# Mamba-2 scan and Hardswish layer: the order of the first loads and of the work up to the feed-forward

## The chip, the cores and the metric

The kernel runs on one core of a Trainium2 chip. The metric is the device time of one execution in microseconds; before the change the median of three runs is 336.48 us (336.34 to 337.1). A profile comes from one further execution, taken by the hardware profiler. Its engines are PE (TensorE; PEld is its weight load), DVE (VectorE), ACT (ScalarE), POOL (GpSimd) and SP (SyncE, which here only issues DMAs). ACT issues DMAs too.

## The reference

Batch 4, 8 heads, sequence 768, head width 32, state width 16, chunks of 32 in the reference. Within a chunk, with `cum` the running sum of log a:

```python
L = np.exp(cum[:, :, :, None] - cum[:, :, None, :]) * causal
y_intra = np.einsum('bhij,bhjd->bhid', np.einsum('bhin,bhjn->bhij', Cc, Bc) * L, xc)
y_inter = np.einsum('bhin,bhnd->bhid', Cc, state) * np.exp(cum)[:, :, :, None]
y[:, :, sl] = y_intra + y_inter
state = decay_full[:, :, None, None] * state + np.sum(Bx, axis=2)
```

The result, as 3072 tokens of 256, goes through a feed-forward layer with 2048 inner columns:

```python
h = x @ w_in
g = h * np.clip(h + 3.0, 0.0, 6.0) / 6.0
return (g @ w_out).astype(np.float32)
```

x, a, B and C are float32; the two weight matrices are float64.

## The kernel before

**Stages.** The sequence is cut into six chunks of 128 positions (`NC = 6`), each for all 4 batches at once, so that a chunk is 512 tokens. Chunk c is scanned (decays, scores, `mix`), and its 512 tokens go through the feed-forward as stage k = c, while the next chunk's scan is woven in. The order of every engine's instructions is written out by hand (`tc.manual_schedule()`): each engine runs its own in the order of the source, and waits where a result is missing. Semaphores are placed by the framework; eight are used for DMAs in turn, so that a ninth DMA waits for the first to land.

**The weights.** `w_in` and `w_out` arrive as float64 bits in eight parts of 1 MB (`load_w`, L144; parts 0 to 3 are `w_in`, 4 to 7 `w_out`), in three buffers `raw`. `decode(i)` (from L190) turns a part into float32: ACT copies the top 16 bits into `ws` (L202), DVE builds the significand in `wm` (L207, L211), masks exponent into `we` and sign into `ws` (L221, L223), ACT maps the exponent in two steps (L227, L230), DVE joins (L234) and multiplies into `w_in` or `w_out` (L244). `decode` is a generator; `weights(i, n)` runs n further pieces of it.

**The head, for chunk 0.** a is loaded first (L83). ACT issues the first weights and B, loads its function table (L150), and then copies and exponentiates; SP issues C in eight loads (`pairs_first`, L103), x (L121), and the second weights. DVE clips a (L284), ACT takes Ln (L286), DVE scans (L289) and splits the sum into three bfloat16 rows in `split` (L296 to L300, `in_three`). PE lays masks in PSUM (L370, L378), and adds differences of sums: `diff_less` (L383) and `diff_pick`, either with sixteen narrow products a batch (L399) or with two wide ones against `spread`, which DVE makes (L279, L391). ACT exponentiates to `L` (L407). C is transposed by DVE (L507) and masked by head (L517), B by PE (L464) with ACT's copy (L473). `scores` (L572) forms C B, `into_state` (L590) B x, `multiply` (L606, L616, L621) copies the state's halves (`adds`, `mid`) and multiplies `L` by the scores, `mix` (L667, L545) gives y, and `keep` (L683) copies it to `yT`. 30 one-column products (L365) and two `busy` products (L535) on PE have no use for the result.

**The first feed-forward stage.** `mlp_in(0, f)` (L693) for f = 0 to 15 multiplies `yT` by 128 columns of `w_in` in two products of 512 columns; the last 18 of the 32 are halved. The four banks f0 to f3 take turns, so that f waits for DVE to be done with f - 4. ACT makes the ramp (L796) and DVE the product `gT` (L801). Parts 2 to 5 are decoded in between: part i is needed from f = 4 i on while i < 4. `first_out` (L814) follows.

Of the kernel before, what the change touches and what calls it, by code (L numbers as in the profile page):

```python
# [21 lines left out]
def kernel(  # L22
# [65 lines left out]
    def load_bc(c):  # L88
# [41 lines left out]
    def load_w(i, queue=nc.sync):  # L130
# [58 lines left out]

    def decode(i):  # L190
# [10 lines left out]
        for sl in (slice(0, n),) if i != 1 else (slice(0, n // 2), slice(n // 2, n)):  # L201
            nc.scalar.copy(out=s[:, sl], in_=top[:, sl])  # L202
            if i == 1 and sl.start == 0:
                yield
# [20 lines left out]
        next(parts_m, None)  # L225
# [5 lines left out]
        if i and i + NRAW < 2 * NP:  # L231
# [23 lines left out]
    spread = [pre[:, 11 + c].bitcast(BF16).rearrange("k (h i) -> k h i", h=NH) for c in range(2)]  # L255
    of_batch = const.tile([P, NB], BF16, name="of_batch")
    of_head = const.tile([P, NH], BF16, name="of_head")
# [4 lines left out]
    def row_signs():  # L262
        with nc.allow_low_precision("zeros and ones"):
# [3 lines left out]
            nc.vector.tensor_reduce(  # L267
                out=of_batch, in_=pick.rearrange("k (b h) -> k b h", b=NB), axis=AX.X, op=ALU.add)
            nc.vector.tensor_reduce(
                out=of_head, in_=pick.rearrange("k (b h) -> k h b", b=NB), axis=AX.X, op=ALU.add)  # L270
# [5 lines left out]

    def spread_rows(c):

        nc.vector.tensor_tensor(  # L279
            out=spread[c], in0=split[:, c].unsqueeze(1).to_broadcast([P, NH, P]),  # L280
            in1=of_head.unsqueeze(2).to_broadcast([P, NH, P]), op=ALU.mult)
# [1105 lines left out]
```

## Time and profile before

| | |
|---|---|
| runs: median (lowest to highest) | 336.48 us (336.34 to 337.1) |
| the profiled execution: its time, its span | 337.3 us, 335.6 us |
| PE, PEld busy | 327.6 us (98%), 272.8 us (81%) |
| DVE, ACT, POOL busy | 264.2 us (79%), 208.2 us (62%), 130.3 us (39%) |
| first L693 product | 21.73 us |
| first L814 product | 49.39 us |
| DVE, ACT busy from 21.73 to 42.30 us | 18.95 us, 18.27 us of 20.57 |
| granted TensorE clock | 1.00 |

The span runs from the first to the last instruction; the device time has 1.7 us more around it. The profile has these views: a page with busy time by engine, slices, DMA queues and the costliest groups; the chain of work that ended last, followed back from the end; waits by engine and line; a timeline, in which neighbours of one kind are merged; and tables by stage with busy time and DMA share. L numbers are lines of the kernel before. A duration of a matmul includes its drain, so that neighbours overlap: the start of the next tells the pace.

### The profile page before, as it was taken

Reading aid. Unit: us, or ns where it says so; the run is one execution under the profiler, and the core shown is the slowest. Engines: PE = TensorE matmul, PEld = TensorE weight load, DVE = VectorE, ACT = ScalarE, POOL = GpSimd, SP = SyncE. Lnnn points to the kernel's source line nnn. Section 1 sums busy time; section 2 is a strip of 40 time slices with the busy share of each in tenths; the row PEclk is TensorE's granted clock in tenths of the full one; section 3 lists DMA queues with packets and bytes.
Section 4 is the critical chain, followed back from the end, with each engine's and each line's share of the span. In section 5 each row is a group of like instructions: output and inputs, shape, how many; then the busy total and the mean of one; then the engine's idle time right before and its main releaser. Section 6 shows DMA issues by size and latency. Waiting matters only on the chain.

```text
span 335.6 us, 8329 instructions
## 1 busy us (share of the span) xinstructions
PE 327.6 (98%) x3361; PEld 272.8 (81%) x3361; DVE 264.2 (79%) x418; ACT 208.2 (62%) x448; POOL 130.3 (39%) x125
## 2 busy tenths in 40 slices
PE   7989999999999999999999999999999999999995
PEld 5554888888888888887888888888888888899995
DVE  6879999879599639869949558938678958599973
ACT  4778887657987570677662577643487221677661
POOL 2200000280743896089973078771058740000000
PEclk9999999999999999999999999999999999999999
DMA  8979960684930214239107258100151001210001
GB/s 174 158 275 212 215 237 9 154 107 126 197 37 4 60 48 109 41 51 96 42 2 163 35 76 77 33 4 11 28 75 14 2 4 17 29 20 0 2 0 63
DMA packets 90181, 25.22 MB, mean 75 GB/s; under 512 B 82784, under 2 KB 86528, under 8 KB 89632
## 3 DMA queue, kind: packets, MB, share of 16 engines
q1 hardware_dynamic: 85760, 23.39, 36.9%
q10 hardware_dynamic: 4384, 1.31, 1.8%
q8 instruction: 26, 0.43, 0.5%
q14 instruction: 11, 0.09, 0.1%
HBM read 21.33 MB, written 3.29 MB: 73 GB/s over the span
## 4 chain that ended last, share of the span: by engine, by line
PE 90%; DVE 4%; DMA 3%; issue 1%; SPq 1%; ACT 1%; DVEq 0%
PE h L757 31%; PE wc L1005 8%; PE wb L1005 8%; PE o L814 8%; PE h L693 8%; PE wa L1005 7%; PE o_end L969 6%; PE wb L1013 3%; PE y L667 3%; PE y L545 2%; DVE q_part L897 2%; DMA raw<-in_moe_w_in_dram 2%; PE cb L572 2%; DVE gT L801 1%; DMA pairs<-in_C_dram 1%
## 5 line engine op out<-in xcount | busy, mean ns | idle before, releaser
L801 DVE SCALAR_TENSOR_TENSOR gT<-gT,h 128x512 f32<-128x512 f32 x96 | 64.7, 683 | 22.0 <-ACT gT L796 20.7
L796 ACT ACTIVATE gT<-h,half 128x512 f32<-128x512 f32 x96 | 65.5, 684 | 24.3 <-PE h L757 21.1
L777 ACT ACTIVATE h<-h 128x512 f32<-128x512 f32 x66 | 38.3, 585 | 37.0 <-PE h L757 36.7
L757 PE MATMUL h<-y_hi,w_part 128*128 128x512 f32 x160 | 50.9, 403 | 0.0
L757 PE MATMUL h<-y_less,w_part 128*128 128x512 f32 x160 | 50.1, 399 | 0.0
L757 PE MATMUL h<-y_lo,w_part 128*128 128x512 f32 x160 | 49.5, 395 | 0.0
L860 POOL TENSOR_TENSOR s<-gT 128x512 f32<-128x512 f32 x16 | 25.3, 1582 | 51.5 <-DVE gT L801 51.5
L757 PEld LDWEIGHTS h<-y_lo,w_part 128*128 128x128 f32 x160 | 30.0, 188 | 6.9
L757 PEld LDWEIGHTS h<-y_hi,w_part 128*128 128x128 f32 x160 | 30.1, 188 | 6.7
L757 PEld LDWEIGHTS h<-y_less,w_part 128*128 128x128 f32 x160 | 29.1, 188 | 6.2 <-DVE h L774 0.3
L427 ACT ACTIVATE L<-L,cum_n 128x64 f32<-128x64 f32 x128 | 31.7, 337 | 1.8 <-POOL L L162 1.8
L814 PE MATMUL o<-w_out,gT 128*128 128x256 f32 x128 | 28.8, 381 | 0.0
L693 PE MATMUL h<-yT,w_in 128*128 128x256 f32 (+1 forms) x100 | 27.8, 440 | 0.0
L814 PEld LDWEIGHTS o<-w_out,gT 128*128 128x128 f32 x128 | 24.1, 190 | 3.4
L693 PEld LDWEIGHTS h<-yT,w_in 128*128 128x128 f32 x100 | 18.9, 190 | 8.6 <-issue 5.7
L860 POOL TENSOR_TENSOR gT<-gT 128x512 f32<-128x512 f32 x16 | 23.9, 1500 | 0.7
L897 DVE TENSOR_TENSOR q_part<-gT,q_part 128x256 fp32r<-128x256 f32 x24 | 21.5, 923 | 0.1
L969 PE MATMUL o_end<-v_pair,g_pair 128*128 128x256 f32 x120 | 21.1, 281 | 0.0
L346 POOL TENSOR_SCALAR cum_n<-cum_t 128x128 f32<-128x128 f32 x1 | 0.5, 534 | 51.9 <-DVE cum_t L344 51.9
L162 POOL TENSOR_SCALAR_AFFINE_SELECT L<-L 64x1024 f32<-64x1024 f32 (+1 forms) x16 | 19.2, 1210 | 3.5 <-DMA L<-cum_d 3.1
L860 POOL TENSOR_TENSOR s<-s,gT 128x512 f32<-128x512 f32 x16 | 20.6, 1292 | 0.0
L438 POOL TENSOR_TENSOR bs<-B,L 128x128 f32<-128x128 f32 x24 | 12.1, 528 | 21.7 <-ACT L L427 14.2
(163 smaller groups left out, 636.2 us busy)
## 6 DMA issues: line engine op xcount, KB each, us to landing
raw<-in_moe_w_out_dram SPq DMA_DIRECT2D x4, 1024.0 KB
L<-cum_d SPq DMA_DIRECT2D x8, 512.0 KB
xt<-in_x_dram SPq DMA_DIRECT2D x6, 512.0 KB
raw<-in_moe_w_in_dram SPq DMA_DIRECT2D x3, 1024.0 KB
out_dram<-back SPq DMA_DIRECT2D x128, 16.0 KB
pairs<-in_C_dram SPq DMA_DIRECT2D x40, 32.0 KB
B<-in_B_dram SPq DMA_DIRECT2D x5, 256.0 KB
eto<-cum_e SPq DMA_DIRECT2D x20, 64.0 KB
```

Source lines behind the costliest of these rows:

```text
L162: nc.gpsimd.affine_select(out=t[rows], in_=t[rows], pattern=pattern, compare_op=ALU.is_ge, fill=-1e5, base=base, channel_multiplier=-1)
L427: nc.scalar.activation(Ls[c][:, b, h], Ls[c][:, b, h], AF.Exp, bias=cum_n[:, c, g:g + 1])
L693: nc.tensor.matmul(out=h[:, t:t + n], lhsT=w_in[f // FP][:, j, f % FP * P:(f % FP + 1) * P], rhs=yTs[k][:, j].rearrange("p b i -> p (b i)" ...
L757: nc.tensor.matmul(out=hs_[k, f], lhsT=w[j][:, f % FP * P:(f % FP + 1) * P], rhs=y[:, j], start=(start and j == 0), stop=True, skip_group_ ...
L777: nc.scalar.activation(h, h, AF.Copy, scale=1.0 / EPS + 1.0)
L796: nc.scalar.activation(gTs[k][:, f], h, AF.Relu, bias=half, scale=1.0 / 6.0)
L801: nc.vector.scalar_tensor_tensor(out=g, in0=g, scalar=1.0, in1=h, op0=ALU.min, op1=ALU.mult)
L814: nc.tensor.matmul(out=o[:, b % 2], lhsT=gTs[0][:, f, b * P:(b + 1) * P], rhs=w_out[:, f], start=(f == 0 and b % 2 == 0), stop=True, skip_ ...
L860: nc.gpsimd.tensor_tensor(out=o, in0=p_, in1=q_, op=op)
L897: nc.vector.tensor_tensor(out=l[:, j], in0=g[:, j], in1=h[:, j].bitcast(FP32), op=ALU.subtract)
L969: nc.tensor.matmul(out=ends_["cross" if n == 2 else "squares"][b], lhsT=g_parts[t][n][:, b * P:(b + 1) * P], rhs=w, start=(t == 0 and b < ...
L1005: nc.tensor.matmul(out=bank[:, slot], lhsT=lhs[:, j], rhs=rhs[:, j], start=(clear and j == 0), stop=True, skip_group_check=True)
```

## The change

Loads. C's first chunk comes in eight loads by head, each 32 rows of 4 batches, odd heads from SP and even heads from ACT, ACT's table load ahead of them. B, the first weights and x follow on SP in this order, all from SP. x's buffer is first written in one column by ACT, after the third exponential of chunk 0, so that x's load waits for that. The second weights' load is moved behind the second of L's four products with the scores (DVE writes one column of its buffer there), and the third weights' load behind the landing of the second's (POOL copies a column from the one buffer to the other).

Order. C is transposed and masked straight after `split`. Every `diff_pick` uses the narrow products, and `spread`, its two sums and both fillers on PE (the 30 thin products and `busy`) go. Chunk 1's differences for batches 0 and 1 stand ahead of the scores, those of 2 and 3 behind them, ahead of `into_state`. The first chunk's B is copied by DVE instead of ACT. `renew(0)` moves from the `first_out` loop to the head. The second weights are decoded in one go ahead of the feed-forward's first factor, with exponent, join and product in two halves of 256 columns (`decode_halves`). No product of `mlp_in` is halved; the first masks are cut differently.

```diff
         def pairs_first(src):
             t = loads.tile([P, 2, NB, 4, N], FP32, name="pairs", tag="bc")
+            if c == 0:
+                for h in range(NH):
+                    rows = slice(h // 2 * 32, h // 2 * 32 + 32)
+                    (nc.sync if h % 2 else nc.scalar).dma_start(
+                        out=t[rows, h % 2].rearrange("s b a n -> s b (a n)"),
+                        in_=src[:, h, sl, :].rearrange("b (s a) n -> s b (a n)", a=4))
+                return t
...
-        Bs[c] = tokens_first(B, nc.scalar if c == 0 else nc.sync, name="B", bufs=1)
         if c == 0:
-            bcs[c] = [pairs_first(C), Bs[c]]
+            bcs[c] = [pairs_first(C)]
+        Bs[c] = tokens_first(B, name="B", bufs=1)
+        if c == 0:
+            bcs[c].append(Bs[c])
...
         xts[c] = loads.tile([P, NB * NH, D], FP32, name="xt", bufs=1)
+        if c == 0:
+            nc.scalar.copy(out=xts[c][:, 0, :1], in_=bias_hi)
...
+        if i == 1:
+            nc.vector.memset(raw[:, :1], 0)
         if i == 2:
-            nc.vector.memset(raw[:, :1], 0)
+            nc.gpsimd.tensor_copy(raw[:, :1], raws[1][:, :1])
         queue.dma_start(out=dst, in_=src)
 
-    load_w(0, nc.scalar)
+    nc.scalar.preload_act_table_set("natural_log_exp_and_others")
     load_bc(0)
-    load_x(0)
-    load_w(1)
-    nc.scalar.preload_act_table_set("natural_log_exp_and_others")
+    load_w(0)
...
+    def decode_halves(i):
...
+        for h in halves:
+            nc.scalar.copy(out=s[:, :, h], in_=top[:, :, h])
+        nc.vector.tensor_scalar(
+            out=m, in0=hi, scalar1=0xFFFFF, scalar2=0x100000,
+            op0=ALU.bitwise_and, op1=ALU.bitwise_or)
+        for h in halves:
+            for t, mask in ((e, 0x7FF0), (s, 0x8000)):
+                nc.vector.tensor_scalar(
+                    out=t[:, :, h], in0=s[:, :, h], scalar1=mask, scalar2=None,
+                    op0=ALU.bitwise_and)
+            nc.scalar.activation(
+                e[:, :, h].bitcast(BF16), e[:, :, h], AF.Relu, bias=bias_hi, scale=-8.0)
+            nc.scalar.activation(
+                e[:, :, h], e[:, :, h].bitcast(BF16), AF.Relu, bias=bias_lo, scale=-1.0)
+        nc.vector.scalar_tensor_tensor(
+            out=m.bitcast(FP32), in0=lo, scalar=2.0 ** -32, in1=m, op0=ALU.mult, op1=ALU.add)
+        load_w(i + NRAW)
+        m = m.bitcast(FP32).rearrange("p (k f) -> p k f", k=NK)
+        for h in halves:
+            nc.vector.tensor_tensor(
+                out=e[:, :, h], in0=e[:, :, h], in1=s[:, :, h], op=ALU.bitwise_or)
+            nc.vector.scalar_tensor_tensor(
+                out=w_in[i][:, :, h], in0=m[:, :, h], scalar=2.0 ** -20,
+                in1=e[:, :, h].bitcast(BF16), op0=ALU.mult, op1=ALU.mult)
...
-        if (c, b) == (0, NB - 1):
-            for _ in range(30):
...
-        n = NH // 4
+        n = NH if c else NH // (2 if b == 0 else 4)
...
     def diff_pick(c, b):
-        if c or b >= 2:
...
-        nc.scalar.copy(out=turned(c)[0], in_=t_ps)
+        (nc.scalar.copy if c else nc.vector.tensor_copy)(out=turned(c)[0], in_=t_ps)
...
+            if c == 0 and q == 1:
+                load_w(1)
...
-            n = TB // (1 + (f * NK + j >= NF * NK - 18))
+            n = TB // (1 + (f * NK + j >= NF * NK - 0))
...
-    for c in range(2):
-        spread_rows(c)
-    diff(0, 0, 1)
-    diff(0, 2, 3)
-    weights(0, 1)
+    turn_squares(bcs[0][0], turned(0)[2])
+    part_heads(0)
+    for b in (0, 2):
+        diff(0, b, b + 1)
     for b in range(NB):
         diff_exp(0, b)
+        if b == 2:
+            load_x(0)
     first_eto()
-    diff(1, 2, 3)
+    turn_b(0)
+    diff(1, 0)
+    diff(1, 1)
     weights(0, 1)
     for b in range(NB):
         ends(0, b)
-    turn_b(0)
-    diff(1, 0, 1)
+    weights(0, 1)
+    scores(0)
+    for b in range(2, NB):
+        diff(1, b)
+        diff_exp(1, b)
     weights(0, 2)
-    diff_exp(1, 2)
-    diff_exp(1, 3)
-    turn_squares(bcs[0][0], turned(0)[2])
-    part_heads(0)
+    own_banks(0)
+    into_state(0, 0, 1)
+    multiply(0)
     fade(0, HALF[1])
     weights(0, 1)
-    busy(2, ps.tile([P, NB * P], FP32, name="d", tag="f3"))
-    scores(0)
-    multiply(0)
+    weights(0, 1)
     load_w(2)
     load_w(3)
-    weights(0, 1)
-    weights(1, 1)
+    renew(0)
     mix(0)
-    keep(0, lambda: weights(1, 1))
-    weights(1, 3)
-    weights(1, 1)
+    keep(0)
+    decode_halves(1)
```

More of the change, by code (lines that the diff above doesn't have):

```diff
@@ L200, in decode @@
         m = att.tile([P, n], U32, name="wm")
[L201 to L204, printed above, removed]
+        nc.scalar.copy(out=s, in_=top)
         def significand():
@@ L362, in diff_mask @@
             d = ps_y.tile([P, NH, HT], FP32, name="d", tag=f"y{b % 2}")
-        if (c, b) == (0, NB - 1):
-            for _ in range(30):
-                nc.tensor.matmul(
-                    out=d[:1, 0, :1], lhsT=ident_h[:, :1], rhs=hide[:, :1], start=True, stop=True,
-                    skip_group_check=True)
-        n = NH // 4
+        n = NH if c else NH // (2 if b == 0 else 4)
         for h in range(0, NH, n):
@@ L388, in diff_pick @@
     def diff_pick(c, b):
-        if c or b >= 2:
-            for a, rows in enumerate(HALF):
-                nc.tensor.matmul(
-                    out=ds[c, b][rows], lhsT=of_batch[:, b:b + 1].to_broadcast([P, HT]),
-                    rhs=spread[c][:, :, rows], start=False, stop=True,
-                    tile_position=(0, a * HT), skip_group_check=True)
-            return
         for h in range(NH):
@@ L530, in turn_all @@
         fade(c)
-    def busy(n, bank):
-        for _ in range(n):
-            nc.tensor.matmul(
-                out=bank[:, :256], lhsT=ident,
-                rhs=ident.unsqueeze(1).to_broadcast([P, 2, P]), start=True, stop=True)
     def from_state(c, a, pairs=range(NQ)):
@@ L565, in scores @@
         cbs[c] = [ps.tile([P, NB, 2, HT], FP32, name="cb", tag=f"f{q}") for q in range(NQ)]
-        if c not in ys:
+        if c not in ys and c:
             own_banks(c)
```

27 lines of the change are left out of this document (11 added, 16 removed).

## The prediction

> **What bounds the kernel now.** I read the engine table first: PE is busy 98% of the span, so little can be won except where PE waits. The chain that ended last, in order of time, shows where that is: from 21.7 us on it is PE, in one piece for tens of us, and ahead of that it is something else. The change touches that head, some weight decoding beside the first feed-forward stage, and the width of 18 products. So the question is when the first L693 product starts (21.73 now), and whether anything stalls the stage later.
>
> The chain of the first 30 us (start, length, what):
>
> ```profile
> 0.79 6.00 DMA raw<-in_moe_w_in_dram
> ...
> 9.18 3.62 DMA pairs<-in_C_dram
> ...
> 14.13 0.89 DVE cT L517 x2
> ...
> 15.16 1.20 PE cb L572 x59
> 16.36 0.84 PE y L590 x50
> ...
> 17.64 0.90 PE y L667 x55
> ...
> 19.42 1.03 issue
> ```
>
> Read it as: C's loads went out late, behind the landing of the first weights (6.79); the last of them landed at 12.80, and transposing, masking and scoring follow. "issue" is 1.03 us in which PE had no wait and nothing to run.
>
> The timeline gives the rows for the sums (start, us, engine, line):
>
> ```profile
> 2.12 1.44 PE L370 MATMUL d<-hide,ident_h 128*128 128x128 bf16 x12 [2.12 <-POOL head L181]
> 3.49 0.89 PE L365 MATMUL d<-hide,ident_h 128*1 128x1 bf16 x30
> ...
> 6.42 1.49 PE L378 MATMUL d<-hide,ident_h 128*128 128x512 bf16 x3
> ```
>
> ```profile
> 9.32 2.21 ACT L407 ACTIVATE L<-d 128x512 f32<-128x512 f32 x4 [1.40 <-PE d L399]
> ...
> 12.93 1.15 ACT L227 ACTIVATE we<-we,bias_hi 128x1024 bf16<-128x1024 uint16 x1
> ...
> 24.92 1.12 ACT L202 COPY ws<-raw 128x1024 uint16<-128x1024 uint16 x1
> ...
> 33.14 1.28 DVE L801 SCALAR_TENSOR_TENSOR gT<-gT,h 128x512 f32<-128x512 f32 x2
> ```
>
> In the second block an exponential takes 0.55 us (2.21/4), half of the exponents' decoding 1.15, and from ACT's copy of the third weights (24.92) to DVE's fifth feed-forward factor (33.14) pass 8.2 us.
>
> **The new path to the first product, step by step.** I call S the end of L300 (6.81 + 0.42 = 7.23), when `split` is ready.
>
> *Ln.* ACT now loads its table first (1.28 us, from 0.79 to 2.07) and then issues four C loads, the last behind a's landing; `less` (0.23) and Ln stand behind them. An issue of 128 packets takes 0.43 (`out_dram<-back`, L1036) to 0.71 us (the first C load), so Ln starts at 4.25 to 5.35 instead of 4.34. I take 0.1 later, nearest the row of the same packet count over 32 rows: S = 7.33.
>
> *PE ahead of S.* The thirty one-column products (3.49 to 4.31) go. Masks and repeats have 5632 columns as before, at 0.43 us for 512: PE is done at 6.8 instead of 7.7, where now L383 waits for the repeats, and S sets its start. A 512-wide product takes 0.43 at 7.70 and 0.22 at 12.25. With the slow pace until 9.0, as now, the first exponential starts at 9.1; with the fast one from S, at 8.5; now 9.32. I take the middle, 8.8.
> [...]
>
> *C and B.* C's last load is issued at about 4.1, and the last one of now landed 3.6 after its issue began, so by 7.7. DVE then transposes (1.12) and masks it (0.89): 9.8, not 15.03. B goes out at 3.2 to 4.3 (a's issue 0.40, four of C's) and the B issued at 68.68 keeps the DMA engines busy until 72.5: landed by 8.5, ahead of its use.
>
> *From the exponentials on.* The third ends at 10.5 (8.8 + 3 x 0.55). B's transposes start 0.22 later (as 11.53 to 11.75) and take 0.66: 11.4; DVE, not ACT, copies them in 0.62 (L621's 2.48/4): 12.05. Two `diff`s of chunk 1, each one wide product and sixteen narrow ones, cost 0.68 apiece (0.22, the 0.31 between such groups, and 16 of L399's 32): 12.6. Scores 1.2: 13.8 (now 16.36). Two more `diff`s with their exponentials behind them: the second ends at 15.9. Then ACT does both halves of the first weights' exponents (2 x 1.15, now at 12.93 and 14.11 and hidden): 18.2. **Only then** come `adds` and `mid`, which PE's `mix` waits for; that is the new wait, and the yT copies stand behind it. `mix` starts 0.42 after `adds` does (17.22 to 17.64): 18.65, and its four pieces take 0.84 + 0.61 + 0.79 + 0.61 = 2.85: **21.5**, if the 1.03 of "issue" goes. It should: the DMA queues by window show one instruction packet between 18 and 19.5, right behind the second weights' burst (371 GB/s from 16 to 18), and that burst now begins after 17.
> x costs nothing here: it goes out behind ACT's mark after the third exponential (0.23, as `less`), at 10.8, and lands 5.2 (that of 248.30 moves data until 253.5) to 6.5 later (issued at 9.79, used by 16.3): 17.3 at most, L590 ends by 18.2, when ACT is free. Beyond that it costs one for one. So the first product moves by -0.23.
>
> *Width of products.* Eighteen products are no longer halved: 4 x 0.216 against 2 x 0.429, 0.005 each: -0.09.
>
> *Weights during the stage.* After B's issue the next one on SP is out 2.95 later (68.68 to 71.63), and a weight load lands 4.9 after its issue ended (13.84 to 18.70): first weights at 11.1 to 12.1. DVE, free of the two `spread` products (2.36), does from 12.05 the significand (1.84), two masks (0.8) and two of L's products (1.24); the second weights go out at 16.05 and land 5.2 later (that of 44.64 moves data until 49.5): 21.3, not 18.7. ACT's copies and pieces for them, 0.6 each, start behind the yT copies at 21.95, all inside the stage now. Third weights: POOL's mark 0.3 and 5.2: 26.8, against ACT's use at 24.92 now. The fifth factor is done 8.6 later (8.2, 0.65 for it, less 0.25 that ACT waited for PE): 35.4. PE wants that bank at 21.5 + 0.1 + 8 x 1.717 = 35.3. **Stall 0.2** (0 to 0.6). After that DVE's pace (6.8 for four) is PE's (6.87): nothing is won back or lost.
>
> *The rest.* `renew` (1.03) leaves DVE's stretch at 63.8, where PE was not waiting: 0. PE's instructions stay as many: +84 narrow, -30 thin, -4, -14 masks, -36 half products. Later stages should look alike.
>
> **Sum:** -0.23 - 0.09 + 0.2 = -0.1 us. The profiled execution took 337.3 (span 335.6 and 1.7 around it): 337.2 there. The median of the runs is 336.48, 0.8 below it: **336.4**.
>
> **Rivals.**
> 1. *Faster.* PE is at full pace from S, and Ln 0.1 early: first exponential at 8.3, first product at 21.0 (-0.73). The weights move with it: second out at 15.6, third in at 26.3, stall 0. With -0.09: -0.8, **335.7**. For it: L399's rows double their pace at 9.0, after 6.9 us of work with a thin stretch. Against: they are slow until then. [...]
> 2. *Slower, by the chain of arrivals.* Each waits for the one before: first weights, DVE's decoding, L's products, second weights, POOL, third weights, ACT in order. It decides from a first landing at 12.9 (beyond 12.05 every us is a us of stall at the ninth f). For it: B's wait on POOL ended at 10.90, 9.6 after its issue, while C shared the queues; if C stretches it by only 2 us, the first weights land at 13.7: stall 1.8, sum +1.5, **338.0**. Against: C's packets are through first.
> 3. *ACT's issues or PE's own supply.* Four issues of 0.71 put Ln at 5.35 (+0.9), or "issue" stays (+1.0): **337.4**. The page counts 26 instruction packets and 0.43 MB, some 16 KB each, and PE's wait for one is the 1.03 above. [...]
> 4. *C comes no sooner.* Then DVE, in order, holds bT and all behind it: masked at 15.0, scored by 16.9, and the new order adds 2.1 + 2.3 + 3.3: 24.6, stall 0.6: **339.8**.
>
> **How the numbers follow.** Forecast 0.40, rivals 0.32, 0.17, 0.07 and 0.04. 0.2% (0.67 us) is about what a measurement of this kernel can tell from no change; the forecast lies inside it, rival 1 below, the others above. The bounds (first exponential 8.3 to 9.1, Ln to +1.0, stall to 0.6) and the rivals give 335.1 to 338.1 for 8 in 10; the low end is rival 1 with a load or two quicker, and what is left out is part of rival 2 and rival 4.
>
> **What would show it.** Scores ending near 13.8; `adds` starting when the first weights' exponents are done, not when L590 ends; no "issue" in L667's products; the first feed-forward product at 21.5; the third weights' copy at 26.8 and a short gap on PE at the ninth f. Wrong would be: x landing after 17.3, first weights after 12.9, or PE waiting for DVE before f = 8.

## The result and the profile after

The changed kernel takes 340.51 us (median of four runs, 339.74 to 340.91), the kernel before 336.61 (336.34 to 337.1) on the same chip: a ratio of 1.0112, 95% interval 1.009 to 1.0134. It is slower by 3.9 us, where 336.4 was forecast with 335.1 to 338.1 around it. The profiled execution took 340.38 us with a span of 338.6 (337.3 and 335.6 before). Line numbers are now those of the changed kernel; those that matter here:

| before | after | what |
|---|---|---|
| L399, L407 | L417, L425 | narrow difference products, exponentials |
| L590, L606 | L601, L617 | `into_state`, `adds` |
| L667, L545 | L680, L556 | `mix`: L times x, C times state |
| L693, L814 | L706, L827 | first feed-forward stage, `first_out` |
| L202, L796, L801 | L246, L809, L814 | copy of weight tops, ramp, `gT` |

The ratio given for the kernel before without thin products leaves out its executions at the lower clock, and the one for the fill of seven leaves out two of its five. The experiments ran on several chips, on which the kernel before took 336.95 to 337.09 instead of 336.61, so that the difference of an experiment to the changed kernel's 340.51 can be some 0.3 to 0.5 too large.

The PE rows of the page's slices, first the busy share and then the granted clock, in tenths:

```profile
PE   7789999999999999999999999999999999999995
...
PEclk9959999999999999999999999999999999999999
```

One slice is 8.5 us. The third one's clock is 5 tenths; before, the row had nothing but nines. The chain of the changed kernel, in order of time (start, length, what), from the last differences on; it lets a product start where the one ahead of it ends, up to 0.2 later than the timeline does, and the text goes by the timeline:

```profile
13.13 0.39 PE d L417 x16
...
13.55 0.60 ACT L L425
14.15 1.04 ACT we L270
...
15.21 1.15 ACT we L273
16.36 0.27 ACT adds L617
...
16.68 1.10 PE y L680 x56
17.77 0.99 issue
18.76 0.44 PE y L680 x8
19.20 1.04 PE y L556 x16
20.25 1.11 PE y L680 x61
21.36 1.05 PE y L556 x16
```

The new wait is where it was expected: `adds` starts when the second half of the exponents is done (16.36). But "issue" is still there (0.99), and behind it each piece of `mix` is slow: the second, sixteen L556, takes 1.04, and the same piece in a run at full clock 0.61. `mix` starts 0.96 sooner than before (16.68 against 17.64) and the first L706 product still comes 0.61 later, at 22.34 in the timeline.

PE and ACT in the timeline (start, length, what; in brackets the idle time ahead of it and who ended it):

```profile
15.23 0.85 PE L601 MATMUL y<-xt,bs 64*32 64x64 f32 x64 [1.73 <-ACT we L270]
...
22.34 30.02 PE L706 MATMUL h<-yT,w_in 128*128 128x512 f32 x64
52.19 8.15 PE L827 MATMUL o<-w_out,gT 128*128 128x256 f32 x37
```

```profile
7.64 1.76 ACT L425 ACTIVATE L<-d 128x512 f32<-128x512 f32 x3 [3.04 <-PE d L417]
...
27.14 1.13 ACT L246 COPY ws<-raw 128x1024 uint16<-128x1024 uint16 x1
```

The first says: PE waited 1.73 us ahead of `into_state`; and 64 L706 products took 29.85 to the start of L827, where 64 x 0.429 is 27.46 (64 records, four to each of the 16 f). Table by stage, on a grid of 3.41 us that the clock's changes lie on (columns: stretch, its length, busy us and count of PE, PEld, DVE, ACT, POOL, then granted clock, DMA share, GB/s):

```profile
13.32:16.73 3.41, 1.09 (x84) 0.84 (x82) 3.38 (x9) 3.28 (x6) 0.00 (x0) 1.00 0.30 44
16.73:20.14 3.41, 2.42 (x80) 1.93 (x80) 2.91 (x6) 0.79 (x3) 0.00 (x0) 0.50 0.86 285
20.14:23.56 3.42, 3.42 (x85) 2.58 (x83) 0.85 (x2) 1.85 (x5) 0.64 (x1) 0.50 0.30 55
23.56:26.97 3.41, 3.41 (x5) 1.34 (x5) 3.31 (x8) 3.35 (x6) 0.00 (x0) 0.50 0.90 354
26.97:30.38 3.41, 3.41 (x10) 1.50 (x9) 2.71 (x6) 2.29 (x4) 0.00 (x0) 1.00 1.02 347
```

In the first stretch PE worked 1.09 of 3.41 us. Then the clock is halved for three stretches, 10.24 us, though PE is busy in two of them from end to end. In the third the L706 products start 0.853 apart, from the stretch behind it on 0.429. (The profile's clock rises at 6.49 and falls at 16.73; the expectations below put the two at 5.92 and 16.16.) The cost: `mix` took 5.66 with 0.99 of "issue" in it, where a run at full clock took 2.80 (`e15_fill10_w2_free` below, 16.75 to 19.55): +1.9. The L706 stage took 29.85 instead of 27.46: +2.4. Together 4.3 us.

### The profile page after: what moved, and what is told of

Read it like the earlier page. It is cut to its first block, busy times and chain, and to the rows that moved or that the text cites. A ratio compares the mean times of both kernels' runs of the same rounds, so it can differ in the third digit from the quotient of the medians.

```text
span 338.6 us, 8337 instructions
## 1 busy us (share of the span) xinstructions
PE 329.6 (97%) x3361; PEld 266.6 (79%) x3361; DVE 263.1 (78%) x419; ACT 208.3 (62%) x450; POOL 129.1 (38%) x126
## 4 chain that ended last, share of the span: by engine, by line
PE 97%; ACT 1%; issue 0%; POOL 0%; DVE 0%; POOLq 0%
PE h L770 33%; PE wb L1018 9%; PE h L706 9%; PE wc L1018 8%; PE o L827 8%; PE wa L1018 8%; PE o_end L982 6%; PE y L680 3%; PE wb L1026 3%; PE y L556 2%; PE cb L583 2%; PE d L395 1%; PE d L417 1%; PE y L601 1%; PE d L408 1%; PE o_end L1000 1%
## 5 line engine op out<-in xcount | busy, mean ns | idle before, releaser
L814 DVE SCALAR_TENSOR_TENSOR gT<-gT,h 128x512 f32<-128x512 f32 x96 | 64.7, 683 | 22.8 <-ACT gT L809 21.4
L809 ACT ACTIVATE gT<-h,half 128x512 f32<-128x512 f32 x96 | 65.6, 685 | 25.1 <-PE h L770 21.3
L706 PE MATMUL h<-yT,w_in 128*128 128x512 f32 x64 | 30.0, 633 | 0.0
L827 PE MATMUL o<-w_out,gT 128*128 128x256 f32 x128 | 28.8, 381 | 0.0
L827 PEld LDWEIGHTS o<-w_out,gT 128*128 128x128 f32 x128 | 24.1, 190 | 3.8 <-issue 0.5
L706 PEld LDWEIGHTS h<-yT,w_in 128*128 128x128 f32 x64 | 13.0, 205 | 16.3 <-issue 15.0
L982 PEld LDWEIGHTS o_end<-v_pair,g_pair 128*128 128x128 f32 x120 | 18.8, 189 | 1.2
L456 POOL TENSOR_TENSOR bs<-B,L 128x128 f32<-128x128 f32 x24 | 10.6, 462 | 19.3 <-ACT L L445 13.9
```

What stands on the lines that cost most here:

```text
L706: nc.tensor.matmul(out=h[:, t:t + n], lhsT=w_in[f // FP][:, j, f % FP * P:(f % FP + 1) * P], rhs=yTs[k][:, j].rearrange("p b i -> p (b i)" ...
L809: nc.scalar.activation(gTs[k][:, f], h, AF.Relu, bias=half, scale=1.0 / 6.0)
L814: nc.vector.scalar_tensor_tensor(out=g, in0=g, scalar=1.0, in1=h, op0=ALU.min, op1=ALU.mult)
L827: nc.tensor.matmul(out=o[:, b % 2], lhsT=gTs[0][:, f, b * P:(b + 1) * P], rhs=w_out[:, f], start=(f == 0 and b % 2 == 0), stop=True, skip_ ...
L982: nc.tensor.matmul(out=ends_["cross" if n == 2 else "squares"][b], lhsT=g_parts[t][n][:, b * P:(b + 1) * P], rhs=w, start=(t == 0 and b < ...
```

## Experiments

Four theories. **1**: PE's wait ahead of L601 halves the clock, and that is the loss. **2**: the clock falls 10.24 us after it rose, whatever PE does. **3**: the clock is a side effect; ACT's order and the chain of held weights set the time. **4**, from the second set of runs on: PE waits for its own code, in pages of 256 instructions. "Granted clock" is the mean of an execution. `mask_again(c, b)` lays the mask of one batch in its bank once more, one product of 512 columns without use.

### Filling the wait, and the fillers of before

`e1_fill`:

```diff
         diff_exp(1, b)
+    for _ in range(5):
+        mask_again(1, 1)
+    diff(1, 1)
     weights(0, 2)
```

> The changed kernel with PE's wait ahead of L601 (13.53 to 15.23 us) filled by work that has no use: chunk 1's masks of batch 1 laid five times over and its differences computed once more, some 1.9 us by the rows of the changed kernel (5 x 0.22, 0.31 and 0.44). Theory 1 (the gap is what makes the clock fall to half at 16.16 for 10.24 us): the record stays at 1.00 from 5.92 on, mix's from_state products take 0.6 and not 1.1, the L706 products start 0.43 apart from the first on, and the time falls by about 4 us, to 336 to 337. Theory 2 (the clock falls 10.24 us after it rose, whatever PE does): half speed from 16.16 again, time 340.5. Theory 3 (the clock is a side effect, and ACT's order and the third weights set the time): less than 1 us gained, and a gap on PE at the ninth f in place of the slow products. By all three 'issue' in mix may move by its 1.0 us, because PE's instructions become 22 more.

346.6 us (343.77 to 348.2), ratio 1.0306, interval 1.0262 to 1.035. Both halves of this result matter. In the profiled execution (343.77) the clock is 1.00 throughout (0.985 to 0.995 in the other three), the first L706 product is at 20.08 and L827 at 49.18, 3.01 sooner than in the changed kernel and 0.21 sooner than before: theory 1 holds that far. But 6.4 us are lost from there on, where nothing was edited. PE's waits (line, who ended them, us in total, times, longest):

```profile
PE y L556 <- issue: 3.0, 2, 1.5
...
PE wb L1026 <- issue: 1.5, 1, 1.5
PE h L706 <- issue: 1.3, 1, 1.3
PE h L770 <- DVE gT L814: 1.1, 1, 1.1
```

The four "issue" waits are at PE's instructions 961, 4033, 5057 and 6081 (every instruction of PE in the trace counted in order of execution, the sequencer's own too), each the 193rd of 256. The fifth wait in the list ended with DVE. In the kernels before and after, the one "issue" wait is at 705, again the 193rd. 22 added products move such a boundary 22 products ahead in the program, here into runs of small products or just behind them. So theory 4 was formed.

`e2_thin` puts the 30 one-column products back:

```diff
     def diff_mask(c, b):
...
+        if (c, b) == (0, NB - 1):
+            for _ in range(30):
+                nc.tensor.matmul(
+                    out=d[:1, 0, :1], lhsT=ident_h[:, :1], rhs=hide[:, :1], start=True, stop=True,
+                    skip_group_check=True)
```

> The changed kernel with the 30 one-column products put back behind chunk 0's fourth mask. Theory 1 (the gap ahead of L601): PE is at half clock longer at the start (record up at about 9.1, not 5.92), so chunk 0's exponentials come some 0.5 later, and the gap ahead of L601 is still there, so the clock falls to half once more near 15.9: 340.5 to 341.5. Theory 2 (10.24 us after it rose): it falls at 19.3 or not at all, because PE is busy there: 336 to 338. Theory 3: no clear change, 340 to 341.

349.99 us (348.81 to 350.66), interval of the ratio 1.0359 to 1.0415. Half clock from 18.59 to 28.83 all the same, as theory 1 has it in kind; and four "issue" waits of 6.5 us in all, at 1985, 4033, 5057 and 6081. The number expected, 340.5 to 341.5, was far off, since it left the pages out.

`e3_before_no_thin` takes those five lines from the kernel before, `e4_before_no_busy` this one:

```diff
-    busy(2, ps.tile([P, NB * P], FP32, name="d", tag="f3"))
```

> The kernel before without its 30 one-column products, all else as it was. Theory 1: the clock rises near 5.9 and not at 9.08; busy and the scores still fill 13.3 to 16.4, so it stays at 1.00; the first products are quicker but C sets the path: 336.0 to 336.6, as before. Theory 2: it falls to half at 16.16 for 10.24 us, mix and six products of the first stage are slow: 339.5 to 341. Theory 3: 336.3 to 336.8.

> The kernel before without its two busy products (13.3 to 14.45, in PE's wait for C), all else as it was. Theory 1 (an idle stretch of 1.7 us ahead of a decision costs the clock): PE is idle from about 12.3 to 15.16, the clock falls to half, from 15.9 or 19.3 on, for 10.24 us: 339 to 341. Theory 2: the rise at 9.08 stays where it is, nothing falls: 336.5. Theory 3: 336.5.

The first: ten executions in two groups, three at 337.27 to 338.26 with a granted clock of 0.998 to 1.0, seven at 345.04 to 347.20 with 0.978 to 0.985. None of the theories expected two groups. The ratio, 1.0022 (1.0005 to 1.0039), is of the first group. The profile, from that group, has no half clock: theory 2, which put the fall at 16.16, is out. The second: 336.78, ratio 1.0001 (0.999 to 1.0012), clock 0.995 to 1.0, although PE waits 2.40 us for C. Theory 1 as worded then, "an idle stretch of 1.7 us costs the clock", fails here. On the grid of this profile the wait is cut in two: PE is busy for 1.91 and for 1.98 us of the two stretches of 3.41 that it lies in, over half of each.

### Moving, releasing and reordering

`e5_move`:

```diff
     turn_b(0)
-    diff(1, 0)
-    diff(1, 1)
...
         diff_exp(1, b)
+    diff(1, 0)
+    diff(1, 1)
     weights(0, 2)
```

> The changed kernel with chunk 1's differences of batches 0 and 1 moved from ahead of the scores to behind those of batches 2 and 3: the same instructions of PE, as many and of the same kinds, now in PE's wait ahead of L601. Scores start when bT is copied (10.4, not 10.9), PE is busy until some 14.4, and about 0.8 of the 1.7 us of waiting is left. Theory 1 (that wait costs the clock): granted clock 1.00, first L706 product near 20.3 (22.34 in the changed kernel), first L827 product near 49 (52.19), time 336 to 336.8. Theory 2 (the clock falls 10.24 us after it rose, in any case): clock 0.983, 340 to 340.5. Theory 3 (ACT's order and the third weights): at most 0.3 of the 3.9 us back, 340.2. Theory 4, from the run with the fill, where five code-fetch waits of 1.1 to 1.5 us appeared behind 22 added instructions: as PE's count is unchanged here, those waits must stay away.

344.13 (343.38 to 345.15), interval 1.0193 to 1.0236. Of the four, only theory 4's rule on the later pages came out. The timeline of PE:

```profile
14.04 0.34 PE L417 MATMUL d<-split,pick 128*64 128x64 bf16 x9
16.16 0.29 PE L417 MATMUL d<-split,pick 128*64 128x64 bf16 x7 [1.78 <-issue]
16.38 0.86 PE L601 MATMUL y<-xt,bs 64*32 64x64 f32 x64
17.70 0.79 PE L680 MATMUL y<-L,xt 64*32 64x64 f32 x56 [0.46 <-ACT adds L617]
22.57 0.44 PE L680 MATMUL y<-L,xt 64*32 64x64 f32 x8 [4.08 <-issue]
```

Nine of sixteen like products run, and the tenth waits 1.78, which the profile puts down to no engine and no data load, at instruction 449; then 4.08 at 705. The DMA queues by window show the 16 KB instruction packets at 13.36 to 14.88 and 20.20 to 21.15; PE goes on 1.3 to 1.4 after such a packet ends. In the changed kernel the first of them ran at 10.44 to 11.48. What went out ahead of them: x at 9.5, whose 4096 packets run from 10.55 to 14.79 there, and the second weights at 15.4 (215 GB/s from 15.5 to 20.1 in this run). So here the first packet begins while such a load runs (in the changed kernel 0.1 ahead of x's), and the second behind one. That the page's wait grows as x goes out sooner is seen further below, in four kernels that issue it at four times.

`e6_free_x`:

```diff
-        if c == 0:
-            nc.scalar.copy(out=xts[c][:, 0, :1], in_=bias_hi)
...
     load_w(0)
+    load_x(0)
...
-        if b == 2:
-            load_x(0)
```

> The changed kernel without the hold on x: no mark by ACT, x's load issued right behind the first weights'. It should land by about 13, so that L601 waits for the exponentials in its banks (14.15) and runs to 15.0; adds still waits for the exponents of the first weights (16.36), so PE waits 0.6 and 1.7 us instead of 1.7 and 0.6. Theory 1: the waiting in the 3.4 us ahead of 16.16 is as long as it was, the clock falls, 340 to 341. If x's hold itself were the cause (L601 late): 337. Theory 3 as theory 1 here, less 0.2: adds starts at 16.36 as before.

344.2 (343.74 to 345.01), interval 1.02 to 1.0235. Theory 1 was 3 to 4 us too low, and the others no nearer. Page 449 comes 2.04 late, page 705 2.18, and half clock lasts 13.65. L600 (the changed kernel's L601) starts 0.09 after the exponential that frees its bank; so in the changed kernel, where it starts 1.08 after it, it waited for x, and the "ACT we L270" in that bracket only ended last by chance. The DMA packets say the same: x's 4096 packets of 128 bytes end at 14.79, 0.44 ahead of L601, and in `e12_w1_free` below the bracket of this wait (1.61) names x's load itself. The hold on x therefore is not waste: with it the packet starts at 10.44 and PE does not wait at 449, without it at 12.57.

`e8_c_one_queue`:

```diff
-                    (nc.sync if h % 2 else nc.scalar).dma_start(
+                    nc.sync.dma_start(
```

> The changed kernel with all eight of C's loads issued by SP. SP then issues nine loads ahead of B (0.4 to 0.7 us each), so C's last lands some 2 us later, near 9.7, DVE holds bT behind cT until some 12, and B, the first weights and x all go out 2 us later. If the second queue is worth what the prediction took it for: scores near 13, first weights near 13.4, adds near 18.3, +1.5 to +2.5 us: 342 to 343. If arrivals did not matter, because PE waits later anyhow: 340.5. On the clock: PE's long wait is then ahead of the scores, so theory 1 has the fall somewhere else or twice; the rise should stay near 5.9.

342.91 (342.58 to 343.47), 2.4 us over the changed kernel (2.0 when each is taken against the kernel before on its own chip): within the 342 to 343 given for a useful second queue, and scores end at 12.9. Part of it is again code (1.42 and 0.47) and clock (0.979 to 0.985).

`e10_all` joins the edits of `e5_move` and `e6_free_x` with this one:

```diff
-    weights(0, 2)
     own_banks(0)
     into_state(0, 0, 1)
     multiply(0)
+    weights(0, 2)
```

> A version meant to beat both kernels: the changed kernel with the differences moved as in the run above, x not held, and the first weights' exponents on ACT (L270, L273) behind adds and mid instead of ahead of them. All PE instructions are kept. Into_state then ends near 15, adds starts right there (16.27 in the changed kernel), mix near 16 as DVE's fourth product is done (16.5 in the changed kernel, some 0.3 sooner here), and the first weights are joined by 20 instead of 18.7. Theory 1: clock 1.00, first L706 product near 20, first L827 near 48.6, 335.5 to 336.3. Theory 2: clock 0.983, 339 to 340. Theory 3: some 1.5 us better than the changed kernel, 339, as the third weights bind.

343.79 (343.63 to 344.88). Pages 449 and 705 are late by 2.05 and 3.01; `adds` starts at 18.02, because L600 does at 16.93. What the new order on ACT is worth can't be seen under these.

### The pages kept in place, and the two other holds

`e11_fill_same_count` is this; `e13_fill_ten_more` leaves the masks' line alone and lays each of the five in two halves (`mask_again(1, 1, NH // 2)`, the width a new parameter):

```diff
-        n = NH if c else NH // (2 if b == 0 else 4)
+        n = NH if c else NH // (2, 1, 2, 4)[b]
...
     diff(1, 0)
-    diff(1, 1)
...
         diff_exp(1, b)
+    for _ in range(5):
+        mask_again(1, 1)
+    diff(1, 1)
     weights(0, 2)
```

> The changed kernel with PE's wait ahead of L601 filled at an unchanged count: chunk 1's differences of batch 1 are moved into it, behind five further layings of their mask that have no use, and five of chunk 0's mask products are saved by cutting two masks less. L601 and all behind it have the place in PE's instructions that they have in the changed kernel. Waits for code have so far all come at the 193rd of each 256 PE instructions (weight loads and products counted); here that gives one, ahead of the last 8 products of L680's first run, as before. Theory 1 (clock): granted clock 1.00, the rest of mix in 2.1 us and not 3.6, the first L706 product near 20.9 (22.34), L827 near 48.5 (52.19), 336 to 336.8, none of the code waits that 22 more instructions brought after 90 us. Theory 4 alone (only waits for code count, the clock follows the time of day): half speed at 16 as before and 340.5.

340.58 (339.29 to 342.12), interval 1.0079 to 1.0147. The later code waits stay away, as expected; the clock does not hold:

```profile
12.71:16.12 3.41, 2.96 (x103) 1.88 (x102) 3.38 (x7) 3.20 (x5) 0.00 (x0) 1.00 0.48 44
16.12:19.53 3.41, 1.52 (x88) 1.14 (x78) 3.34 (x7) 1.31 (x5) 0.00 (x0) 1.00 0.80 257
19.53:22.95 3.42, 3.42 (x93) 2.67 (x89) 1.16 (x3) 1.60 (x5) 0.64 (x1) 0.50 0.25 72
```

The filled stretch (2.96 busy) passes; the one behind it, with 0.46 for `adds` and 1.43 of "issue", has 1.52 of 3.41 busy and is followed by half clock. With the wait ahead of L601 nearly gone (0.45), the fall came with the one for code as the larger part, 1.43 of these 1.89 us.

> As the run above, but the filling masks are ten products of half the width and nothing is saved: PE has 10 products more ahead of L601. Theory 4: the fetch of a code page is asked for some way into the page ahead, and in the changed kernel that place lies behind L601, which waits for x until 15.23; with ten products more it may be reached while PE is still filling, so the page comes some 1.4 us sooner and the 0.99 of 'issue' in mix shrinks or goes: first L706 product near 20, L827 near 47.6 if nothing in the weights binds. Later pages begin ten products earlier: the three code waits after 90 us that 22 more brought (1.1 to 1.5 each) are each smaller by about ten products of 0.1 to 0.23, so 0 to 0.5. Clock 1.00. 335.3 to 337.

341.64 (340.07 to 343.47), interval 1.0104 to 1.0185; the two quicker executions have clock 1.00. In the profiled one there is no "issue" in `mix` and the first product is at 19.47, 2.87 sooner than in the changed kernel, as theory 4 said. The instruction packet is out at 14.28, ahead of L601; in the changed kernel at 16.38, 1.15 after L601 began. With five and seven products more (below) it still is 1.1 behind L601, with ten it isn't. The first instruction of L601 is the 15th of its page in the changed kernel, the 25th, 29th and 35th with five, seven and ten products more: so, as an estimate from these four runs, the packet comes once PE is past a place between the 29th and the 35th, and a wait of PE ahead of that place puts it off. The place itself isn't shown. And then theory 3 comes in, which no run had shown until here. PE's timeline (L708 is L706 moved by two lines), and the chain of the same execution:

```profile
19.47 7.13 PE L708 MATMUL h<-yT,w_in 128*128 128x512 f32 x16
26.98 1.98 PE L708 MATMUL h<-yT,w_in 128*128 128x512 f32 x4 [0.37 <-DVE gT L816]
30.92 5.29 PE L708 MATMUL h<-yT,w_in 128*128 128x512 f32 x11 [1.96 <-DVE gT L816]
```

```profile
15.52 5.59 DMA raw<-in_moe_w_in_dram
...
21.23 0.65 POOL raw L156
...
21.90 6.54 DMA raw<-in_moe_w_in_dram
...
28.46 1.10 ACT ws L246
29.56 0.60 ACT gT L811
```

Second weights, POOL's mark, third weights, ACT's copy of them, and only then the ramp that the sixth f waits for. With 0.48 more at the ninth f, PE is idle for 2.8 us in the stage; by starts the stage takes 31.48, 4.0 more than its 27.46, and L827 is at 50.95. `e1_fill` has the same hold and full clock, but its third weights are copied at 26.68 instead of 28.46, and PE does not wait at the sixth f.

`e12_w1_free` releases the second weights, `e14_w2_free` the third (two diffs, one below the other):

```diff
-        if i == 1:
-            nc.vector.memset(raw[:, :1], 0)
...
             load_x(0)
+            load_w(1)
...
-            if c == 0 and q == 1:
-                load_w(1)
```

```diff
         if i == 2:
-            nc.gpsimd.tensor_copy(raw[:, :1], raws[1][:, :1])
+            nc.vector.memset(raw[:, :1], 0)
```

> The changed kernel without the hold on the second weights: no mark by DVE, the load issued right behind x's (near 10 us instead of 15.4). Theory 4 (code waits behind data): the code page that PE asks for between 13 and 15 finds 1 MB of weights in the queues, as in the runs without x's hold, where such a page came 2 to 4 us late: PE waits 2 to 3 us more in mix, the half clock lasts longer, 342 to 344. Theory 3 (the chain of weight arrivals binds): the second weights land near 17.5 instead of 20.9, the third ones 3 us sooner, and the time falls by up to 0.5: 340.

> The changed kernel with the third weights' load no longer held behind the landing of the second's: the mark is DVE's (as in the kernel before) instead of POOL's copy, so that load goes out near 18.7 instead of 21.7. Theory 4: one code page is fetched at 19.5 to 20.4 in the changed kernel, and PE is at its own 961st instruction only near 33 us, so a delay of it costs nothing: 340.5. Theory 3: third weights 2 to 3 us sooner, and since no gap on PE was left in the stage, 340.5 too. If the hold itself cost something: 339 to 340.

The first: 341.9 (341.41 to 342.49), 1.4 over the changed kernel; "issue" in `mix` is 2.24. Theory 4's direction, but less than its number: 1.25 us more of waiting where 2 to 3 were expected. The second: 341.06 (339.78 to 343.51), interval 1.0095 to 1.0199, no difference that four runs show. Under half clock the hold shows no cost.

`e15_fill10_w2_free`, `e16_fill5_w2_free` and `e17_fill7_w2_free` join that release of the third weights with ten, five (`mask_again(1, 1)` five times) and seven products more (two of the five in halves):

> The run with ten more products in PE's wait, and beside that the third weights' load held by DVE's mark alone (as in the kernel before), not behind the second's landing. Alone, without the fill, that hold cost nothing. If it binds once PE is quick: third weights in near 24.5 instead of 28.4, the 2.0 us that PE waited at the sixth f goes, L827 starts near 48.2 instead of 51.12, and the time is 338 (341.6 with the hold), of which 1.2 us are the two code waits at 179 and 227. If PE's waits there came from DVE's order and not from the landing: 341.

> As the run with ten, with five whole masks: PE has five products more than in the changed kernel. The pages that begin near 179 and 227 begin five products later than with ten, five products of 0.22 further on, so those two waits (0.55 and 0.62 with ten) go. L601 stands five products further into its page than in the changed kernel: if that is enough for the next page to be asked for while PE fills, mix has no code wait (0.99 in the changed kernel), the first L706 product is near 19.6, L827 near 48, and the time 335.5 to 336.5, below the kernel before. If not, mix waits some 1.4 us, the clock falls in part of the runs, and it is 338 to 340.

> As the run with five, with seven products more (two of the five masks in halves). If the page behind L601 is asked for at a place between five and seven products, this run has no code wait in mix where that with five has one: 335.5 to 336.7, at most 0.3 of code waits near 179 and 227. If both have it or neither, the two differ by less than 0.5.

With ten, the profiled execution (337.64) is what was expected to a few tenths:

```profile
19.55 14.00 PE L708 MATMUL h<-yT,w_in 128*128 128x512 f32 x32
34.01 14.00 PE L708 MATMUL h<-yT,w_in 128*128 128x512 f32 x32 [0.46 <-DVE gT L816]
47.85 13.98 PE L829 MATMUL o<-w_out,gT 128*128 128x256 f32 x64
```

L827's place (here L829) is at 47.85, 3.10 sooner than with the hold and 1.54 sooner than in the kernel before; the one gap, 0.46, is at the ninth f; two code waits near 175 and 223 (0.81 and 0.60) give most of that back. But only two of six executions are so (337.64 and 338.37, clock 0.998 and 0.999); four have 0.99 and 341.48 to 342.25. Seven: seven executions at 336.46 to 337.99 with 0.998 to 1.0, five at 341.17 to 341.90 with 0.99 (the ratio of 1.0044, interval 1.0012 to 1.0076, takes in three of these five; the seven alone have a mean of 337.29, where the kernel before has 337.02). Five: one at 337.61 (0.999), five at 340.48 to 341.37 (0.988 to 0.99), and the profile has the code wait in `mix` (1.43). One kernel, two times, some 4 us apart: this is the plainest sign of what the clock costs. The clock itself accounts for about 3 of the 4 (0.009 of 338); a longer code wait can be the rest, which isn't shown, as each kernel has the profile of one execution. None beats the kernel before (336.51 to 337.52 beside them).

`e18_x_after_second`, `e19_x_after_first` and `e20_fill_x_second` release x one or two exponentials sooner (`b == 1`, `b == 0`), the third weights as in `e14_w2_free`; the last with the fill of `e11_fill_same_count`:

> The changed kernel with x released behind the second exponential instead of the third, 0.55 us sooner, and the third weights held by DVE's mark only (alone that cost and gained nothing). PE's instructions are untouched. If x's landing ends PE's wait: x in near 14.5, L601 near 14.6, the wait 1.1 and not 1.73, the code page behind it 0.6 sooner, so that less than half of the clock's 3.4 us is waiting and the granted clock stays 1.00: first L706 product near 20.2, L827 near 48, 335.5 to 336.5. If x's packets get ahead of the code page fetched from 9.9 on (as they did without the hold), PE waits 1 to 2 us inside the differences and the clock falls: 341 to 344. If neither: 340.5.

> As the run with x behind the second exponential, behind the first: out at some 8.4, in near 14. L601 then waits for the exponentials in its banks until 14.15, as without the hold. If the code page fetched at 9.9 still gets through: 335 to 336.5, clock 1.00. More likely x's packets are ahead of it, the page is late by 1 to 2 us, and the time is that of the run without the hold: 343 to 344.5.

> x behind the second exponential, the third weights held by DVE's mark only, and chunk 1's differences of batch 1 moved into PE's wait behind five layings of their mask, at an unchanged count of products. PE is then busy until L601 at 14.9, the page behind it is asked for 0.4 sooner than in the fill at unchanged count, and its wait in mix (1.43 there) is about 1.0: waiting in the 3.4 us that decide is 0.5 + 1.0, below half, clock 1.00 in most runs: L827 near 48, 335.5 to 336.5. If the page stays as late: clock 0.99 and 340, as there.

340.28, 340.70 and 340.14 (intervals within 1.0058 to 1.013), clocks 0.983 to 0.993. x went out at 9.01, 8.45 and 8.84 instead of 9.50, and L601 started at 15.47, 15.65 and 15.59 instead of 15.23: releasing x sooner does not land it sooner. It follows the first weights, which were issued at 3.98 and are copied at 11.38, through the queues: x's first packet starts at 10.5 to 10.8 and its last ends at 14.8 to 15.2, whether it was issued at 9.50, 9.01, 8.84, 8.45 or, in `e6_free_x`, at 6.63. So the mark by ACT is not what makes PE wait; by these starts x's place behind 1 MB of weights is. x ahead of the first weights wasn't tried. What the mark goes with is seen in the instruction packet near there: x issued at 9.50, 9.01, 8.45 and 6.63 (`e6_free_x`) has that packet start at 10.44, 10.79, 11.44 and 12.57, and PE waits for page 449 by 0, 0, 0.59 and 2.04.

## Why the prediction was wrong, point by point

- *Ln, C and B, the exponentials.* Each was sized too late, and what happened lies beyond rival 1's numbers: PE was at full pace from 6.49, ACT's four issues (0.81 to 3.49) ran beside its table load (0.78 to 2.06), Ln began at 3.68 (forecast 4.44), the first exponential at 7.64 (8.8, bounds 8.3 to 9.1), scores ended at 12.12 (13.8), the halves of the exponents at 16.36 (18.2). `mix` began at 16.68 instead of 18.65. Up to there the forecast is 2.0 us too late.
- *"It should: the 1.03 of issue goes."* **Failed.** It came to 0.99. The forecast took the packet to be late because of the second weights' burst. But the packet starts only at 16.38, 1.15 after L601 did (15.23); PE goes on 3.5 after L601's start (18.76), and is there after 2.5. Behind a burst the wait was longer (4.08 in `e5_move`, after 215 GB/s from 15.5 to 20.1), but a quick packet doesn't heal it: in `e11_fill_same_count` it took 0.95, near the least of any (0.88), and PE waited 1.43.
- *"its four pieces take 0.84 + 0.61 + 0.79 + 0.61".* **The step that failed.** The sum took these pieces, and the 64 products behind them at 0.429, from rows at full clock. The forecast asked only from when on PE would have its full pace, and let it stay. Filling removed (`busy`, the thin products) and a wait added ahead of L601 left PE 1.09 of 3.41 us of work, and half clock made `mix` 1.9 dearer and the L706 stage 2.4. No term or rival had this.
- *x costs nothing here.* Half right. x was there by 15.23, ahead of 17.3, and with L590's successor done at 16.08 `adds` did wait for ACT. But ACT was 1.8 early too, so PE stood 1.73 us, and behind this wait came the packet of 16.38 and, from 16.73 on, half clock.
- *Width, third weights, the ninth f.* Third weights were copied at 27.14 (26.8), no gap at the ninth f. The term was not refuted, it was covered: with PE at full pace the same chain left PE idle for 2.8 us (`e13_fill_ten_more`), and for 0.46 when its last hold was gone, then at the ninth f as forecast. Rival 2 was right as a mechanism in that run and came on the sixth f first, by way of ACT's order.
- *The rest: later stages look alike.* Yes: 286.5 us from L827's start to the span's end, 286.2 before. The count of PE's products, 3361 in both, which the forecast noted for its cost only, goes with it: 22 or 30 more cost 6.4 and 8.8 us there (`e1_fill`, `e2_thin`), of which code waits are 4.5 and 6.5.

Sum, on the profiled executions (forecast 337.2, measured 340.38): start of `mix` -2.0, "issue" +1.0, half clock +4.3, the stall not seen -0.2; together +3.1, and 3.2 is the difference.

Would the change have paid without the clock's fall? 340.38 less 4.3 is 336.1, 1.2 below before's 337.3, if nothing else were behind it. `e13_fill_ten_more` shows that something can be: with the hold on the third weights, L827 starts at 50.95 even at full clock, later than before's 49.39, and its two executions at clock 1.00 took 341.26 and 340.07, as long as the changed kernel (1.2 of the 341.26 are two later code waits). In `e1_fill`, with the same hold, it started at 49.18, so how much the hold costs depends on when the weights land. No run at full clock was clearly quicker than the kernel before. Of the change's parts, then, C's second queue gains (2.0 to 2.4, code waits included), x's and the second weights' holds pay by keeping code pages on time (3.3 to 3.7 and 1.0 to 1.4), and the third weights' hold can cost once PE is quick (3.1, between two profiled executions).

## What to carry to other kernels

Filler on PE and the place of a load in a queue can be doing a job that the page doesn't name: before removing the one or moving the other, look at PE's idle time around it (here in stretches of 3.41 us) and at the granted clock. In these runs small products used up PE's code faster than it came (64 of L601 run in 0.85 us, so that the 128 of a page take some 1.7, where PE went on with its next page only 3.5 after L601 began), and 22 products more brought 4.5 us of waits to stages that nobody touched (`e1_fill`, near 177, 226 and 278); compare variants at an unchanged count. When a head gets quicker, the chain of arrivals behind it has to get quicker too, and a slow clock can hide that it doesn't: here 2.8 us of waits in the first feed-forward stage came up only at full clock (`e13_fill_ten_more`).

## What the runs showed of the hardware that was not expected

**The clock's grid.** In the profiles, its changes lie 3.41, 6.83, 10.24, 13.65 or 17.07 us apart, multiples of 3.41, and the grid lies differently in each execution (it first shows full speed at 5.16 to 9.07). In all 20 profiled executions, on that grid, half clock followed each stretch at full clock in which PE was busy for less than half, 15 of them with 0 to 1.64 us, and none in which it was busy for 1.73 or more; this leaves out the kernel's last stretches. There, where PE's work runs out, six were at 1.47 to 1.69 and full clock followed all the same (1.56 in `e11_fill_same_count`, from 333.56 on). So half clock does not go by busy time, as the profile counts it, alone; what else counts isn't shown. The two nearest half ahead of the end, of `e20_fill_x_second` (half clock follows) and of `e13_fill_ten_more` (it doesn't):

```profile
15.58:19.00 3.42, 1.64 (x120) 1.33 (x121) 3.38 (x7) 1.94 (x4) 0.00 (x0) 1.00 0.54 129
```

```profile
27.23:30.64 3.41, 1.73 (x4) 0.42 (x3) 0.46 (x1) 2.18 (x3) 0.00 (x0) 1.00 1.02 399
```

In the head it came back at the end of the first stretch with 2.9 us or more of L706 products; 2.63 (`e2_thin`) did not do, nor did a stretch full of `mix`'s smaller products alone (`e2_thin`, 18.59 to 22.00). The differing grid would explain two groups of times in one kernel; that was not tried by itself. Two things stay open: all ten executions of `e4_before_no_busy` kept 0.995 or more with a wait of 2.40 us, which a grid at random should have caught in some (two of them have 0.995, and 0.005 of 336 us, 1.7, is what one stretch at half clock costs); and the lower group of `e3_before_no_thin` lost 8 to 9 us, where 1.5 to 2.2% of the clock are 5.2 to 7.6 us.
In the stretch ahead of the fall, no single wait was longer than 1.73 us in the changed kernel and than 1.43 in `e11_fill_same_count`: ahead of the kernel's end it is the idle time of a stretch in sum, 2.32 of 3.41 and 1.89 of 3.41, that went with the fall.

**Code.** Of 35 "issue" waits of over 0.3 us on PE in the 20 profiles, 34 are at an instruction that is the 193rd of 256 (the other, in `e6_free_x`, is ahead of L600, where the exponentials end). The 16 KB packet ahead of such a wait takes 0.9 to 2.1 us, and PE goes on 0.9 to 1.6 after it. These waits lasted 0.5 to 4.1 us where small products follow each other. In the profiles of the kernels before and after, PE has 6752 instructions, 26.4 times 256, and there are 26 such packets. In the changed kernel one runs from 27.14 to 28.08, while PE is at its 927th to 931st instruction, and there is no "issue" wait at the 961st.
